# Closing weights' parts, block 0's splits and the last product of a fused attention and expert kernel: a change of order

## The chip, the cores and the metric

One core of a Trainium2 chip runs the whole kernel. The metric is the device time of one execution in microseconds (us). The engines are TensorE (PE, with its weight loads PEld), VectorE (DVE), ScalarE (ACT), GpSimd (POOL) and SyncE (SP), which here only issues DMAs. Each engine works through its own instructions in the order of the program and waits for others by semaphores.

## The reference

Three layers on 1536 tokens of 512 numbers, all in float32:

```python
attn = retention(q, k, v, lam)            # 2 x 8 heads x 768 x 64, blocks of 64 with decay
x = attn.transpose(0, 2, 1, 3).reshape(1536, 512)
logits = x @ w_gate                       # 8 experts
P = exp(logits - logits.max())
for _ in range(8):                        # Sinkhorn: rows, then columns
    P /= P.sum(1, keepdims=True) + 1e-09
    P /= P.sum(0, keepdims=True) + 1e-09
    P *= 1536 / 8
for e in range(8):                        # every token through every expert
    out += P[:, e:e + 1] * (relu(x @ w1[e]) @ w2[e])     # 512 -> 1024 -> 512
h = out @ w_in                            # 512 -> 2048
return (h - tanh(h)) @ w_out              # 2048 -> 512
```

## The kernel before, in words

Every float32 product is three products of halves: a factor is split into a high part (an ACT copy to fp32r, `split` with `which` 0) and a low part (a subtraction on DVE or POOL, `which` 1), both at L176 and L178, and high x high, low x high and high x low are added up in PSUM.

**Attention** takes some 60 us. **The expert layer** is a loop over 64 **slots** (from L838): a slot is one quarter of the hidden units of one expert (`q`) for one half of the tokens (`b`, six tiles of 128). The first matrix product of a slot is done by a scheme with seven block products (1, 2, 5, 6, 7, 4, 3 in that order on TensorE) on sums of blocks, and sums of the results; between them stands the second matrix product of the slot before, `tiles(s - 1, ...)`, six tiles, three after product 6 and three after product 7 (L617 to L641). DVE adds each tile to `yacc` at L641. The slot begins with ACT's copy `sa<-pal` (L858) of product 1. The relu of a result is an ACT copy (L679: `h0h`, `h1h`) and a DVE remainder (L680: `h0l`, `h1l`). Product 5 of the next slot goes into a PSUM bank that `h1l<-pal` of this slot was the last to read.

**Other work is hung into the slots** in four lists: `fd` runs behind the issue of product 5 and ACT's copy of it, ahead of product 6 and ACT's copy `sb`; `fa` behind product 7 and DVE's addition `pah`; `fb` behind the last tiles, ahead of the relu of `pah`; `fc` at the slot's end. The position sets an instruction's place in its engine's queue. The lists hold the expert weights (a load of `wraw` by SP in `fc`; POOL's `w_sum` in `fa` of even slots; `w1_split` in `fd` and `fa` and `w2_split` in `fb` of odd slots, with remainders of the last two on POOL), the gate and Sinkhorn in the early slots, the scaling `scale0` in slots 7 to 9, and the **conversion of the closing weights** in slots 5 to 60. These come as float64, in 64 pieces `n` of 128 x 256. `conv(u, i, j)` (L563) does step `j` of a piece:

- j = 0: SP loads the piece into a ring of three (`d`).
- j = 1: five DVE operations (L580 to L587, all on SBUF) and two POOL operations (L588, L589) make a float32 of it in a ring of seven.
- j = 2: two DVE operations (L591, L592).
- j = 3: a piece p = n % 8 of the second four, or one of the first three, is split into a high and a low **part** (`block`: an ACT copy and a POOL subtraction `hl` into a ring of five) and a write to the scratch memory `wscr` is noted in `stores`; for p = 3 POOL makes two sums instead.
- j = 4 and 5 (after p = 3 only): two parts each; j = 4 also two POOL sums.

`flush` issues the noted writes on SP's queue: at the start of each `conv` step those of earlier slots, and all of them where its argument is true. A piece has j = 0 in `fa`, j = 1 in `fa` of the next slot and j = 2 in its `fc`. In ten slots (10, 16, 22, 26, 32, 38, 42, 48, 54, 58) a second piece has j = 0 in `fd`, j = 1 in `fb` and j = 2 in the next slot's `fd`. The hanging is written out at L790 to L800.

**The closing layer** (from L960) runs 24 groups (3 blocks of 512 tokens, 8 quarters) of seven block products on 128 x 256 blocks `f`, with the function h - tanh(h) made on ACT and DVE in steps (`unit`), ending in a high part (`hi`, L952, ACT) and a low part (`lo`, L954, DVE, `gl`); `second` is the last matrix product. Block 0's input is made in slot 63 and after it: `turn` transposes, and `x2_parts` makes the sums (DVE, L716) and splits (ACT copy `x2h`, remainder `x2l`) in the order that calls at L802 to L807, L890, L892 and L973 give. The output tiles are evacuated by ACT and DVE in turn and written by `evac` (L662).

Of the kernel before, what the change touches and what calls it, by code (L numbers as in the profile page):

```python
# [17 lines left out]
B, H, S, D = 2, 8, 768, 64  # L18
E, DM, FE, FF = 8, 512, 1024, 2048
N = B * S  # L20
CH = 128
# [6 lines left out]
TPB = BT // 128  # L28
NU = 2 * E
NQ = FF // 512  # L30
# [6 lines left out]
NS = len(SLOTS)  # L37
# [18 lines left out]
def kernel(  # L56
# [85 lines left out]
    for g, (b, j) in enumerate(order):  # L142
        at_ = [w for w, (p, _) in kept.items() if p == j]
# [396 lines left out]
    def flush(all=False):  # L540
        while stores and (all or stores[0][0] < now[0]):
            stores.pop(0)[2]()
# [19 lines left out]

    def conv(u, i, j):  # L563
        q, p = 2 * u + i // 8, i % 8
        flush(j == 2)
        if j == 0:
            d = cq.tile([128, NC64, 2], I32, tag=f"d{count[2] % 3}", name=f"d{u}_{i}")
            count[2] += 1
            nc.sync.dma_start(out=d.rearrange("p n t -> p (n t)"),
                              in_=wio[u].bitcast(I32)[:, i * 2 * NC64:(i + 1) * 2 * NC64])  # L570
            c0 = cp.tile([128, NC64], I32, tag="c0", name=f"c0_{u}_{i}")
            box[q, p] = [d, c0]
            return
        if j == 1:
            box[q, p].append(cq.tile([128, NC64], I32, tag=f"c1_{count[0] % 7}", name=f"c1_{u}_{i}"))
            count[0] += 1
        d, c0, c1 = box[q, p]
        hi, lo, val = d[:, :, 1], d[:, :, 0], c1.bitcast(F32)
        if j == 1:
            nc.vector.tensor_scalar(out=c0, in0=hi, scalar1=3, scalar2=0x40000000,  # L580
                                    op0=ALU.logical_shift_left, op1=ALU.bitwise_xor)
            nc.vector.tensor_scalar(out=c1, in0=hi, scalar1=-0x80000000, scalar2=None, op0=ALU.bitwise_and)
            nc.vector.scalar_tensor_tensor(out=c0, in0=c0, scalar=0x7FFFFFFF, in1=c1,
                                           op0=ALU.bitwise_and, op1=ALU.bitwise_or)
            nc.vector.tensor_scalar(out=val, in0=lo.bitcast(U32), scalar1=2.0 ** -52,
                                    scalar2=None, op0=ALU.mult)
            nc.vector.tensor_scalar(out=lo, in0=c0, scalar1=-0x800000, scalar2=None, op0=ALU.bitwise_and)  # L587
            nc.gpsimd.tensor_tensor(out=val, in0=val, in1=lo.bitcast(F32), op=ALU.mult)  # L588
            nc.gpsimd.tensor_tensor(out=val, in0=val, in1=c0.bitcast(F32), op=ALU.add)  # L589
        elif j == 2:  # L590
            nc.vector.tensor_scalar(out=lo, in0=hi, scalar1=0x7FFFFFFF, scalar2=None, op0=ALU.bitwise_and)  # L591
            nc.vector.scalar_tensor_tensor(out=val, in0=lo.bitcast(F32), scalar=thr, in1=val,  # L592
                                           op0=ALU.is_ge, op1=ALU.mult)
        elif j == 3:
            if p < 3:
                block(q, (0, 256, 1536)[p], val)
            elif p == 3:
                a11, a22 = (box[q, k][2].bitcast(F32) for k in (0, 2))
                nc.gpsimd.tensor_tensor(out=a22, in0=val, in1=a22, op=ALU.add)
                nc.gpsimd.tensor_tensor(out=val, in0=a11, in1=val, op=ALU.subtract)  # L600
            else:
                block(q, 1792 + 256 * (p - 4), val, True)
        elif j == 4:
            a11, a12, a22 = (box[q, k][2].bitcast(F32) for k in range(3))
            block(q, WI[5], a22)
            block(q, WI[7], val)
            nc.gpsimd.tensor_tensor(out=a11, in0=a22, in1=a11, op=ALU.subtract)
            nc.gpsimd.tensor_tensor(out=a12, in0=a12, in1=a11, op=ALU.subtract)
        else:
            a11, a12 = (box[q, k][2].bitcast(F32) for k in range(2))  # L610
            block(q, WI[6], a11)
            block(q, WI[3], a12)
# [49 lines left out]
    def evac(b, t):  # L662
        if t == 0:
            yacc[b] = yp_.tile([128, TPB, DM], F32, tag=f"y{b}", name=f"yout{b}")
        y = yacc[b][:, t]
        if t % 2 == 0:
            nc.scalar.activation(out=y, in_=ypsum[b, t], func=ACTF.Copy)
        else:
            nc.vector.tensor_copy(out=y, in_=ypsum[b, t])
        n0 = t % B * S + (b * TPB + t) // B * CH  # L670
        (nc.scalar if t % 2 == 0 and b == NBLK - 1 else nc.sync).dma_start(out=out[n0:n0 + 128, :], in_=y)

    def scale0(c):
# [60 lines left out]
    fd, fa, fb, fc = spots  # L734

    def put(f, s, what, *a):
        f[s].append(lambda: what(*a))
# [51 lines left out]
    n = 0  # L789
    for s in range(lo_, hi_):  # L790
        more = s % 2 == 0 and (s - lo_) // 2 * extra // ((hi_ - lo_) // 2) != ((s - lo_) // 2 + 1) * extra // ((hi_ - lo_) // 2)
        for steps in (((fa, s - 1), (fa, s), (fc, s)), ((fd, s), (fb, s), (fd, s + 1)))[:1 + more]:
            for j, (f, at_) in enumerate(steps):
                put(f, at_, conv, n // (nconv // NQ), n % (nconv // NQ), j)
            at_ = (at_, at_ + 1)[f is fc]
            put(fa, at_, conv, n // (nconv // NQ), n % (nconv // NQ), 3)
            if n % 8 == 3:
                for j in (4, 5):
                    put(fa, at_ + j - 3, conv, n // (nconv // NQ), n % (nconv // NQ), j)
            n += 1  # L800
    assert n == nconv
    for k in range(KT):  # L802
        if k == 2:
            put(fb, NS - 1, x2_parts, (1, 0), (1, 1), 5)
        put((fa, fb)[k // 2], NS - 1, turn, 0, k)
    put(fb, NS - 1, x2_parts, (5, 0))
    put(fc, NS - 1, x2_parts, (5, 1), (2, 0), (2, 1), (3, 0))  # L807


    def product(ps, s, i, start):  # L810
# [78 lines left out]
    tiles(NS - 1, (0,))  # L889
    x2_parts(7, (3, 1))  # L890
    tiles(NS - 1, (1,))
    x2_parts(6, (6, 0), (6, 1))  # L892
    tiles(NS - 1, (2,))

    glos = [xp2.tile([128, 512], F32R, name=f"gl{i}") for i in range(2)]
# [66 lines left out]
    for g in range(ng):  # L962
        f = [bank(f"f{i}_{g}") for i in range(2)]
        ph[g, 0], ph[g, 1] = f
        c11, c12, c21, c22 = f[0][:, 0:256], f[0][:, 256:512], f[1][:, 0:256], f[1][:, 256:512]
        cproduct(g, c21, 1, True)
        nc.scalar.activation(out=s1, in_=c21, func=ACTF.Copy)
        unit(g - 1, 1, "t", "th", "q1")
        cproduct(g, c11, 2, True)
        unit(g - 1, 0, "p2")  # L970
        nc.vector.tensor_tensor(out=c11, in0=c11, in1=s1, op=ALU.add)
        if g == 0:
            x2_parts((7, 0), (7, 1), 4, (4, 0), (4, 1))  # L973
        unit(g - 1, 0, "cp")
        unit(g - 1, 1, "w", "sub")
        unit(g - 1, 0, "hi")
        unit(g - 1, 1, "q2")
        if g == 0:
            tiles(NS - 1, (3,))
        elif g == 1:  # L980
            turn(2, 0)
            turn(2, 1)
        seconds(g - 2, 1, (0, 1))
        unit(g - 1, 0, "lo")
        unit(g - 1, 1, "w1", "p2")
        cproduct(g, c12, 5, True)
        nc.scalar.activation(out=s1, in_=c12, func=ACTF.Copy)
        cproduct(g, c21, 6, False)
        nc.scalar.activation(out=s2, in_=c21, func=ACTF.Copy)
        unit(g - 1, 1, "mk")  # L990
        b, j = g // NG + 1, g % NG - 1
        if b < NBLK and j >= 0:
            if b == 2 and j == 0:
                x2_alloc(2)
            x2_step(b, j, nc.gpsimd)
        if g == 0:
            for k in range(KT):
                turn(1, k)
        elif g == 1:
            turn(2, 2)  # L1000
            turn(2, 3)
        seconds(g - 2, 1, (2, 3))
        for n, (_, _, p) in enumerate(loads):
            if p >= 0 and p == g - 2:
                w2_load(n)
        cproduct(g, c21, 7, False)
        nc.vector.tensor_tensor(out=c22, in0=c21, in1=s1, op=ALU.add)
        cproduct(g, c12, 3, False)
        nc.vector.tensor_tensor(out=c12, in0=c12, in1=s2, op=ALU.add)
        unit(g - 1, 1, "cp")  # L1010
        unit(g, 0, "t", "th")
        unit(g - 1, 1, "hi")
        unit(g, 0, "q1", "q2", "mk", "w")
        unit(g - 1, 1, "lo")
        unit(g, 0, "sub", "w1")
        if g == 0:
            tiles(NS - 1, (4,))
        seconds(g - 1, 0, (0, 1))
        cproduct(g, c21, 4, False)
        for n, (_, _, p) in enumerate(loads):  # L1020
            if p >= 0 and p == g:
                w1_load(n)
        if g == 0:
            tiles(NS - 1, (5,))
            w2_load(2)
        seconds(g - 1, 0, (2, 3))
    g = ng - 1
# [8 lines left out]
    second(g, 0, range(TPB), (0, 1))  # L1036
    second(g, 0, range(TPB), (2,))
    unit(g, 1, "hi", "lo")
    second(g, 1, range(TPB), (0, 1))
    for t in range(TPB):  # L1040
        second(g, 1, (t,), (2,))


# [43 lines left out]
```

## Time and profile before

| | |
|---|---|
| median of 3 runs | 1264.67 us (1263.93 to 1264.79) |
| the profiled execution | 1266.17 us, of which its span, first to last instruction, 1264.4 us |
| granted TensorE clock, mean | 0.999 |
| busy: DVE, ACT, POOL | 1022.3 us (81%), 591.7 (47%), 531.8 (42%) |
| DMA | 141.83 MB, 112 GB/s in the mean |
| largest waits of SP | for POOL's `w2l` 327.2 us (30 times), for DVE's `w1l` 229.9 (31), both ahead of the loads of `wraw`; for POOL's `hl` 135.2 (38), ahead of writes |

Busy shares are of the span. A time in the trace is in us from the span's start; durations of matmuls overlap, since they are pipelined, and a stretch between the starts of two of them tells the pace. "[3.78 <-DMA wscr<-hl]" behind a row means that the engine was idle for 3.78 us before it, and what ended that.

### The profile page before, as it was taken

To read this page: it belongs to the slowest core of one execution; us is meant where nothing else is said; L and a number is where in the kernel's file an instruction comes from. 1 tells how busy PE (TensorE), PEld (TensorE's weight loads), DVE (VectorE), ACT (ScalarE), POOL (GpSimd) and SP (SyncE) were. 2 spreads that over 40 slices of the span, in tenths; PEclk is the share of its full clock that TensorE was granted. 3 is DMA by queue.
4 is the path that set the end of the run, shared out by engine and by line. 5 is a ranking of instruction groups with operands and counts; after the bars stand their busy time and mean duration, and the time that the engine had idled before them with its cause. 6 is when DMAs were issued, how large, how long until landed. Compare 5 with 4: busy or idle time off the path is not lost. (4 is left out here: it accounts for less than half of the span.)

```text
span 1264.4 us, 20257 instructions
## 1 busy us (share of the span) xinstructions
PE 1237.5 (98%) x7450; PEld 1139.8 (90%) x7450; DVE 1022.3 (81%) x1914; ACT 591.7 (47%) x1191; POOL 531.8 (42%) x696
## 2 busy tenths in 40 slices
PE   8999999999999999999999999999999999999997
PEld 6889998899999999989999999999989899999996
DVE  6978888877888887887787888887785688888987
ACT  5653333333333433333333443333333378888875
POOL 4843444544554545554554554554452022031000
PEclk9999999999999999999999999999999999999999
DMA  9311122322222333232232222232325267284571
GB/s 332 121 34 42 51 67 67 109 68 75 84 84 76 95 109 105 76 95 81 76 100 76 84 83 76 67 102 87 111 57 194 92 205 254 101 276 150 198 260 67
DMA packets 63634, 141.83 MB, mean 112 GB/s; under 512 B 6064, under 2 KB 33200, under 8 KB 63536
## 3 DMA queue, kind: packets, MB, share of 16 engines
q1 hardware_dynamic: 63104, 140.02, 33.5%
q8 instruction: 58, 0.95, 0.3%
q10 hardware_dynamic: 432, 0.53, 0.1%
q14 instruction: 40, 0.33, 0.1%
HBM read 114.32 MB, written 26.21 MB: 111 GB/s over the span
## 5 line engine op out<-in xcount | busy, mean ns | idle before, releaser
L641 DVE SCALAR_TENSOR_TENSOR yacc<-yq,prob,yacc 128x512 f32<-128x512 f32 x336 | 239.5, 744 | 95.9 <-PE yq L628 95.4
L178 POOL TENSOR_TENSOR w1l<-wsum,w1h 128x256 fp32r<-128x256 f32 x124 | 88.6, 745 | 179.0 <-ACT w1h L176 164.8
L626 PE MATMUL yq<-w2h,h1h 128*128 128x512 f32 x384 | 146.2, 381 | 1.1 <-ACT h1h L679 1.1
L628 PE MATMUL yq<-w2h,h1l 128*128 128x512 f32 x384 | 145.7, 379 | 0.0
L627 PE MATMUL yq<-w2l,h0h 128*128 128x512 f32 x384 | 145.6, 379 | 0.0
L628 PE MATMUL yq<-w2h,h0l 128*128 128x512 f32 x384 | 145.6, 379 | 0.0
L626 PE MATMUL yq<-w2h,h0h 128*128 128x512 f32 x384 | 145.6, 379 | 0.0
L627 PE MATMUL yq<-w2l,h1h 128*128 128x512 f32 x384 | 145.6, 379 | 0.0
L818 PE MATMUL pal<-xsl,w1h 128*128 128x384 f32 x384 | 125.3, 326 | 0.5 <-DVE xsl L178 0.5
L816 PE MATMUL pal<-xsh,w1h 128*128 128x384 f32 x384 | 125.6, 327 | 0.0
L819 PE MATMUL pal<-xsh,w1l 128*128 128x384 f32 x384 | 125.2, 326 | 0.0
L679 ACT ACTIVATE h1h<-pah 128x384 fp32r<-128x384 f32 x64 | 31.3, 490 | 172.5 <-PE yq L627 161.2
L178 POOL TENSOR_TENSOR w2l<-wraw,w2h 128x512 fp32r<-128x512 f32 x64 | 82.7, 1313 | 6.5 <-ACT w2h L176 6.5
L588 POOL TENSOR_TENSOR c<-c,d 128x256 f32<-128x256 f32 x64 | 47.4, 740 | 88.8 <-DVE d L587 85.1
L628 PEld LDWEIGHTS yq<-w2h,h1l 128*128 128x128 f32 x384 | 72.6, 189 | 10.6 <-DVE h1l L680 0.4
L627 PEld LDWEIGHTS yq<-w2l,h0h 128*128 128x128 f32 x384 | 72.6, 189 | 10.3
L626 PEld LDWEIGHTS yq<-w2h,h0h 128*128 128x128 f32 x384 | 72.7, 189 | 10.2
L628 PEld LDWEIGHTS yq<-w2h,h0l 128*128 128x128 f32 x384 | 72.6, 189 | 10.2
L626 PEld LDWEIGHTS yq<-w2h,h1h 128*128 128x128 f32 x384 | 72.6, 189 | 8.3 <-ACT h1h L679 1.4
L864 ACT ACTIVATE sa<-pbh 128x384 f32<-128x384 f32 x64 | 31.4, 491 | 102.1 <-DVE pbl L862 90.0
L129 POOL TENSOR_TENSOR wsum<-wraw 128x256 f32<-128x256 f32 x31 | 22.6, 730 | 134.3 <-DMA wraw<-in_w 134.3
L627 PEld LDWEIGHTS yq<-w2l,h1h 128*128 128x128 f32 x384 | 72.7, 189 | 6.8
(228 smaller groups left out, 3680.3 us busy)
## 6 DMA issues: line engine op xcount, KB each, us to landing
wraw<-in_w SPq DMA_DIRECT2D x64, 512.0 KB, 5.0
wscr<-hl SPq DMA_DIRECT2D x88, 256.0 KB, 5.7
d<-in_wio SPq DMA_DIRECT2D x64, 256.0 KB, 5.4
w1h<-wscr SPq DMA_DIRECT2D x18, 768.0 KB, 4.5
w1l<-wscr SPq DMA_DIRECT2D x18, 768.0 KB, 6.0
w2h<-wscr SPq DMA_DIRECT2D x18, 512.0 KB, 3.8
w2l<-wscr SPq DMA_DIRECT2D x18, 512.0 KB, 4.8
qk<-in_qkv SPq DMA_DIRECT2D x11, 512.0 KB, 8.2
```

The lines of the kernel that those rows point to most:

```text
L129: eng.tensor_tensor(out=s1, in0=a21, in1=a22, op=ALU.add)
L178: eng.tensor_tensor(out=lo, in0=src, in1=hi.bitcast(F32), op=ALU.subtract)
L588: nc.gpsimd.tensor_tensor(out=val, in0=val, in1=lo.bitcast(F32), op=ALU.mult)
L626: nc.tensor.matmul(out=yp, lhsT=hi, rhs=pairs(w2h[q][:, i]), start=i == 1, stop=False)
L627: nc.tensor.matmul(out=yp, lhsT=hi, rhs=pairs(w2l[q][:, i]), start=False, stop=False)
L628: nc.tensor.matmul(out=yp, lhsT=lo, rhs=pairs(w2h[q][:, i]), start=False, stop=i == 0)
L641: nc.vector.scalar_tensor_tensor(out=y, in0=yp, scalar=prob[:, c, q // 4:q // 4 + 1], in1=y, op0=ALU.mult, op1=ALU.add)
L679: nc.scalar.activation(out=hi, in_=ps, func=ACTF.Relu)
L816: nc.tensor.matmul(out=ps, lhsT=w1h[q][:, ws], rhs=pairs(xh[:, k]), start=start and k == 0, stop=False, skip_group_check=True)
L818: nc.tensor.matmul(out=ps, lhsT=w1h[q][:, ws], rhs=pairs(xl[:, k]), start=False, stop=False, skip_group_check=True)
L819: nc.tensor.matmul(out=ps, lhsT=w1l[q][:, ws], rhs=pairs(xh[:, k]), start=False, stop=k == 1, skip_group_check=True)
L864: nc.scalar.activation(out=sa, in_=pbh, func=ACTF.Copy)
```

## The change

Three things are put elsewhere; no instruction is added or taken away.

1. Steps j = 3, 4 and 5 of a piece go from `fa` to `fd` of the same slot, those of a second piece from `fa` to `fb`. All noted writes are issued at step j = 1 (in `fa` or `fb`) instead of j = 2.
2. Block 0's splits: ACT's copy (5, 0) goes from `fb` to `fc`, where the copies (2, 0) and (3, 0) now stand ahead of the remainders (5, 1) and (2, 1); the split of sum 6 goes from ahead of the last slot's third tile to behind the first addition (`c11`) of group 0.
3. The very last product runs tile by tile, three matmuls each, instead of the two `hi` matmuls of all four tiles and then the four `lo` matmuls. The line of `n0` in `evac` moves up; it is arithmetic of the host.

```diff
     def conv(u, i, j):
         q, p = 2 * u + i // 8, i % 8
-        flush(j == 2)
+        flush(j == 1)
...
         for steps in (((fa, s - 1), (fa, s), (fc, s)), ((fd, s), (fb, s), (fd, s + 1)))[:1 + more]:
             for j, (f, at_) in enumerate(steps):
                 put(f, at_, conv, n // (nconv // NQ), n % (nconv // NQ), j)
-            at_ = (at_, at_ + 1)[f is fc]
-            put(fa, at_, conv, n // (nconv // NQ), n % (nconv // NQ), 3)
-            if n % 8 == 3:
-                for j in (4, 5):
-                    put(fa, at_ + j - 3, conv, n // (nconv // NQ), n % (nconv // NQ), j)
+            f, at_ = (fd, at_ + 1) if f is fc else (fb, at_)
+            for j in (3, 4, 5) if n % 8 == 3 else (3,):
+                put(f, at_ + j - 3, conv, n // (nconv // NQ), n % (nconv // NQ), j)
             n += 1
...
-    put(fb, NS - 1, x2_parts, (5, 0))
-    put(fc, NS - 1, x2_parts, (5, 1), (2, 0), (2, 1), (3, 0))
+    put(fc, NS - 1, x2_parts, (5, 0), (2, 0), (3, 0), (5, 1), (2, 1))
...
     tiles(NS - 1, (1,))
-    x2_parts(6, (6, 0), (6, 1))
+    x2_parts(6)
     tiles(NS - 1, (2,))
...
         if g == 0:
-            x2_parts((7, 0), (7, 1), 4, (4, 0), (4, 1))
+            x2_parts((6, 0), (6, 1), (7, 0), (7, 1), 4, (4, 0), (4, 1))
...
     unit(g, 1, "hi", "lo")
-    second(g, 1, range(TPB), (0, 1))
     for t in range(TPB):
-        second(g, 1, (t,), (2,))
+        second(g, 1, (t,))
```

## Rows read from the trace of the kernel before

**Rows 1.** The page's busy times: busy us, share of the span, instructions.

```profile
PE 1237.5 (98%) x7450; PEld 1139.8 (90%) x7450; DVE 1022.3 (81%) x1914; ACT 591.7 (47%) x1191; POOL 531.8 (42%) x696
```

**Rows 2.** Waits of TensorE: us in total, times, longest us.

```profile
PE pbh L816 <- DVE h1l L680: 8.5, 10, 1.7
```

**Rows 3.** Timeline of ACT: start and duration of L858 in slots 7, 14, 19, 61.

```profile
155.56 0.49 ACT L858 ACTIVATE sa<-pal 128x384 f32<-128x384 f32 x1 [1.76 <-PE pal L819]
...
262.36 0.49 ACT L858 ACTIVATE sa<-pal 128x384 f32<-128x384 f32 x1 [1.52 <-PE pal L819]
...
335.33 0.49 ACT L858 ACTIVATE sa<-pal 128x384 f32<-128x384 f32 x1 [1.51 <-PE pal L819]
...
956.48 0.49 ACT L858 ACTIVATE sa<-pal 128x384 f32<-128x384 f32 x1 [1.52 <-PE pal L819]
```

**Rows 4.** Timeline of slot 42: its start on ACT, and `h0l` on DVE.

```profile
676.57 0.49 ACT L858 ACTIVATE sa<-pal 128x384 f32<-128x384 f32 x1 [1.52 <-PE pal L819]
...
686.47 0.54 DVE L680 SCALAR_TENSOR_TENSOR h0l<-pbl,h0h 128x384 fp32r<-128x384 f32 x1
```

**Rows 5.** Timeline of slot 32 and the start of product 5 of slot 33.

```profile
526.85 0.49 ACT L858 ACTIVATE sa<-pal 128x384 f32<-128x384 f32 x1 [1.52 <-PE pal L819]
...
529.06 1.92 SPq L551 DMA_DIRECT2D wscr<-hl  x3
...
530.37 0.48 ACT L867 ACTIVATE sb<-pal 128x384 f32<-128x384 f32 x1
...
533.40 0.33 PE L816 MATMUL pal<-xsh,w1h 128*128 128x384 f32 x1
...
535.25 0.61 ACT L176 ACTIVATE hl<-c 128x256 fp32r<-128x256 f32 x1 [3.78 <-DMA wscr<-hl]
...
536.22 2.48 POOL L178 TENSOR_TENSOR hl<-c,hl 128x256 fp32r<-128x256 f32 x3
...
538.79 0.53 DVE L680 SCALAR_TENSOR_TENSOR h0l<-pbl,h0h 128x384 fp32r<-128x384 f32 x1
...
543.92 0.43 PE L816 MATMUL pbh<-xsh,w1h 128*128 128x384 f32 x1 [1.60 <-DVE h1l L680]
```

**Rows 6.** L583 and tile `hl` (ns min/median/max; DMA in us); two page groups (busy, mean, idle).

```profile
L583 DVE SCALAR_TENSOR_TENSOR c<-c,c x64: 424/426/891, 152.0 to 937.1; 128x256 int32<-128x256 int32 x64
...
L176 ACT ACTIVATE hl<-c x88: 407/418/612, 162.2 to 945.9; 128x256 fp32r<-128x256 f32 x88
L178 POOL TENSOR_TENSOR hl<-c,hl x88: 724/812/1097, 165.5 to 951.3; 128x256 fp32r<-128x256 f32 x88
...
DMA to landing us min/median/max: 2.4/5.7/7.5
...
L641 DVE SCALAR_TENSOR_TENSOR yacc<-yq,prob,yacc 128x512 f32<-128x512 f32 x336 | 239.5, 744 | 95.9 <-PE yq L628 95.4
...
L129 POOL TENSOR_TENSOR wsum<-wraw 128x256 f32<-128x256 f32 x31 | 22.6, 730 | 134.3 <-DMA wraw<-in_w 134.3
```

**Rows 7.** Timeline from slot 63 to group 0; then a window: engines' busy us, PEclk, DMA.

```profile
1000.47 0.75 ACT L176 ACTIVATE x2h<-raw 128x512 fp32r<-128x512 f32 x1 [0.79 <-DVE raw L716]
...
1002.03 0.48 PE L626 MATMUL yq<-w2h,h1h 128*128 128x512 f32 x1 [1.08 <-ACT h1h L679]
...
1008.27 0.87 ACT L176 ACTIVATE x2h<-raw 128x512 fp32r<-128x512 f32 x1 [4.62 <-DVE raw L716]
...
1010.92 0.38 PE L915 MATMUL f<-x2h,w1h 128*128 128x256 f32 x1 [1.86 <-DVE f L971]
...
1011.90:1015.90 4.00, 4.00 (x24) 4.00 (x23) 0.91 (x2) 1.96 (x5) 1.60 (x3) 0.57 0.00 0
```

**Rows 8.** Timeline of the end; landing of the output writes (us).

```profile
1256.29 0.69 DVE L954 TENSOR_TENSOR gl<-un_raw,h1l 128x512 fp32r<-128x512 f32 x1 [0.70 <-ACT h1l L952]
...
1258.13 1.03 PE L658 MATMUL yp<-w2h,gl 128*128 128x512 f32 x4
...
DMA to landing us min/median/max: 2.0/2.8/4.3
```

More of the change, by code (lines that the diff above doesn't have):

```diff
@@ L665, in evac @@
         y = yacc[b][:, t]
+        n0 = t % B * S + (b * TPB + t) // B * CH
         if t % 2 == 0:
@@ L669, in evac @@
             nc.vector.tensor_copy(out=y, in_=ypsum[b, t])
-        n0 = t % B * S + (b * TPB + t) // B * CH
         (nc.scalar if t % 2 == 0 and b == NBLK - 1 else nc.sync).dma_start(out=out[n0:n0 + 128, :], in_=y)
```

## The prediction

> **What bounds the kernel.** I read the busy table first: TensorE is busy 98% of the span [rows 1], so the time is its work plus the little that it waits. The list of its waits comes next: after the attention part the largest is `pbh` (product 5) waiting for the DVE remainder `h1l`, 8.5 us in 10 slots [rows 2]. The starts of the slots give the full price. Slots 7 to 60, which hold the conversion of the closing weights, take 956.48 - 155.56 = 800.92 us; the undisturbed slots 14 to 18 take 72.97 us, 14.594 each [rows 3]. 54 x 14.594 = 788.1, so **12.8 us** are lost in the conversion slots (a stalled product also refills its pipeline, hence more than 8.5).
>
> Slot 32 shows how [rows 5]. SP issues the three writes of slot 31's parts late, at 529.06, behind the weight load. ACT then wants to copy a new part into the same ring of five, and waits 3.78 us for a write to land; the relu copy `h0h` stands behind it. POOL's three remainders `hl` (2.48 us) run beside DVE's five conversion operations. DVE reaches `h0l` only 11.94 us after the slot's start (526.85 to 538.79), everything behind it is late, and product 5 of the next slot waits 1.60 us. So in a slot with two conversions `h0l` may start 10.3 us in (11.94 - 1.60); with one conversion some 1.7 later, as five DVE operations fewer stand behind it (below). Slot 42, also with two, reaches it after 9.90 us and its successor waits for nothing [rows 4].
>
> The DVE operations themselves show the second half. L583, one of the five, reads and writes SBUF and takes 0.42 us at best, 0.89 at worst [rows 6]; in slot 32 it ran inside POOL's three `hl`. L641, which reads PSUM, takes 0.74 in the mean of 336 [rows 6]. The other four of the five have one SBUF input; I put them at 0.3 to 0.35 undisturbed and all five at 1.7. One `hl` of 0.81 us beside the five operations thus costs DVE about 0.4.
>
> **The change, part by part.**
>
> *Parts behind product 5, writes in mid-slot.* No instruction is added. The ACT copies (0.42 each), POOL remainders (0.81 each) and POOL sums of a part move from behind the `pah` addition (fa) to behind product 5 (fd), some 4 to 5 us earlier; those of a slot's second conversion go behind tile 5 (fb). POOL has them done before the five operations start, unless it has much else: ahead of each `wsum` it now waits 134.3 us in 31 for the weights [rows 6], 4.3 a time. The writes move in SP's queue from behind `wraw`'s load to ahead of the next `d` load. SP now waits there for `hl`, and the `d` load behind it has until the next slot's five operations, a whole slot against a few us: cost nothing. A write landed 5.7 us after issue in the median, 7.5 at most [rows 6]; issued 5 to 9 us into a slot it is down by 17, and the copy that needs its ring place comes at about 14.6 + 3. So the waits of ACT (slots 12, 32, 52) go.
>
> What lies under the new place: ACT's `sb` copy comes up to three copies later, 3 x 0.42 = 1.3 us. In slot 32 it ended at 530.85 and product 7, which may overwrite `pal` only then, started at 533.40 [rows 5]: 2.55 us of cover. DVE in fd mostly reads PSUM; its weight remainders in odd slots read SBUF and may be slowed by some 0.4 to 0.8, while DVE waits 0.78 before each of the following sums (95.4 us in 122 waits) [rows 6].
>
> What stays: POOL's four `wsum` operations (0.73 each [rows 6]) come when `wraw` lands, and the moved work can push them into the five. Three parts with two sums take 3 x 0.81 + 2 x 0.75 = 4.0 us of POOL, from about 2.9 (after ACT's `sa` and the first copy) to 6.9; `wsum` then runs to 9.8, and the five start at 8.2 (slot 42's 9.90 less 1.7): 1.6 us of overlap, 0.8 of delay, `h0l` at 10.7, 0.4 past what slots with two conversions allow. I leave 0.4 each in slots 10, 38 and 58, 0.4 in 11 (POOL full there), 0.2 in 32, and 1.0 for the rest, above all slots 9 and 10 with block 0's scalings, which the change leaves: 2.8 of 12.8 remain, **gain 10.0 us**. Bounds: 4.6 if only the landing waits and what hangs on them go (slots 12, 13, 32 and 52), 12.8 if all goes.
>
> The rule that speaks against this is in the Trainium skill, "SBUF — State Buffer", section "SBUF: two separate sides": VectorE and GpSimd share a pair of ports as an exclusive lock, and whoever comes second is blocked for the other's whole instruction. L583's doubling agrees. By the rule the moved remainders would block DVE's weight remainders just as they blocked the five operations; what that gives is a rival below.
>
> *Block 0's sums and splits.* (a) ACT's copy `x2h` at 1000.47 waits 0.79 for a DVE sum and holds `h1h` back; TensorE then waits 1.08 [rows 7]. Behind the relus, that copy costs them nothing: gain 1.1. Three copies instead of two now stand ahead of `h0h` of the last slot, needed only for tiles 3 to 5; cover enough. (b) The copy at 1008.27 (0.87) and its remainder stand ahead of the first group's addition, for which TensorE waits 1.86 [rows 7]. Moved behind it, the addition loses 0.7 of remainder and about 0.9 of waiting for ACT in front: 1.6 of the 1.86. The remainder is next wanted by product 6 of group 0, one product later (0.7 us): 0.1 to 0.2 may come back. Net of both, 2.8. (c) From 1011.9 to 1015.9 the granted clock was 0.57, a mixture of full and half (2.4 and 1.2 GHz) [rows 7]; it fell right after the 1.86 of idleness and cost 4.00 x 0.43 = 1.7. With 0.3 to 0.5 idle I take it to stay up: the mean clock of 0.999 leaves no room for falls after the slots' waits of 1.6 us. What follows on DVE hangs on the group's additions and moves along. **Gain 4.5 us**, bounds 2.0 ((a), half of (b), the clock falls anyway) and 5.4.
>
> *Last product tile by tile.* Before, eight matmuls need only `h1l`, and four `gl` ones follow from 1258.13 at 0.215 spacing, so all four tiles end within 0.65 us and four writes queue up [rows 8]. After, the third matmul needs `gl`, which DVE has at 1256.29 + 0.69 = 1256.98; TensorE would be there at 1258.13 - 6 x 0.215 = 1256.84, so it loses 0.2. Tiles end 0.65 apart; the last evacuation no longer queues behind another (about 0.2), and the last write goes out alone: writes of this kind landed in 2.0 us at best, 2.8 in the median [rows 8], 0.8 less. **Gain 0.8 us**, bounds 0 and 1.3. The moved `n0` line is host arithmetic: nothing.
>
> **Sum.** 10.0 + 4.5 + 0.8 = 15.3. The profiled execution took 1266.17 with a span of 1264.4; it stands 1.50 over the median of the runs. Its span would be 1249.1, its time 1250.9; against the median, 1264.67 - 15.3 = **1249.4 us**.
>
> **The rivals.**
> *The window fills again.* POOL is delayed by the same work earlier, and `wsum` and `w1l` slide into the five operations, which stay doubled. For: POOL's work per slot is unchanged and in the fullest slots reaches past 8.2 us. Against: in slots with one part it is done with that long before. Only the landing waits go, 4.6: 1264.67 - 9.9 = 1254.8. Chance 0.14.
> *The clock falls anyway* in the first group, as DVE and ACT feed it sparsely there: 1.7 less, 1251.1. For: two waits remain possible. Against: the only fall seen follows the longest wait. 0.07.
> *The port lock in the new place.* Odd slots: one `hl` holds the weight remainder for up to 0.81; against it stand three waits of 0.78 on DVE, so it shows only where DVE is already late (39, 59 and 11): 3 x 0.81 = 2.4 less, 1251.8. The skill's page just named would have it so. 0.03.
> *Slower.* The copies in fd still meet a write that has not landed, and now `sb` stands behind them. With a wait like 3.78 and 1.3 of copies against 2.55 of cover, product 7 loses 2.5 us. It decides from six such slots on (15.3 / 2.5); in the twelve slots with three parts it would cost 30: 1279. Against: the writes go out half a slot earlier. 0.03.
> *Nothing comes of it*: DVE's work is the same and each stall moves to the next wait; 1264. Against: slot 42. 0.03.
>
> **How the numbers follow.** The forecast has the remaining 0.70. The sum of the upper bounds, 12.8 + 5.4 + 1.3 = 19.5, gives 1245.2; that of the refilled window with poor ends, 4.6 + 2.6 + 0.5 = 7.7, gives 1257.0. A measurement here tells about 0.2%, 2.5 us, from no change. Faster 0.94, same 0.03, slower 0.03.
>
> **What would show it.** Slots 10 to 13, 32/33, 38 to 40 and 58 to 60 near 14.6 us; no ACT wait of `hl` on a write; L583's maximum seen rarely; `h0l` about 10 us into every slot. No wait of TensorE above 0.5 at the first group and a clock of 1.00 there. Evacuations 0.65 apart at the end. Wrong would be TensorE waiting for `sb` at product 7, or the five DVE operations still near 3.5 us in total.

## The result and the profile after

The kernel after takes **1250.79 us** in the median (1250.11 to 1251.02, 4 runs), the kernel before 1264.47 beside it (1263.93 to 1264.79, 4 runs): a ratio of 0.9891, 95% interval 0.9874 to 0.9908. It is 13.7 us faster; 15.3 were forecast. The profiled execution of after is the fastest of its four, 1250.11 with a span of 1248.3. Below the change, line numbers of after are 3 lower.

The page's busy times, beside [rows 1]:

```profile
PE 1233.6 (99%) x7450; PEld 1138.0 (91%) x7450; DVE 995.8 (80%) x1914; ACT 589.8 (47%) x1191; POOL 536.9 (43%) x696
```

The counts of instructions are those of before. DVE does the same 1914 operations in 26.5 us less: some of them became shorter. TensorE's waits, beside [rows 2] (us in total, times, longest):

```profile
PE yp L655 <- ACT h1l L949: 1.1, 1, 1.1
PE pbh L813 <- DVE h1l L680: 0.9, 3, 0.4
...
PE f L912 <- DVE f L968: 0.5, 2, 0.3
```

The 8.5 us at product 5 have become 0.9, the 1.86 at the first group's addition 0.3, and the wait for `h1h` is gone from the list. The timeline of ACT at slots 7 and 61, beside [rows 3]:

```profile
155.04 0.49 ACT L855 ACTIVATE sa<-pal 128x384 f32<-128x384 f32 x1 [1.76 <-PE pal L816]
...
945.80 0.49 ACT L855 ACTIVATE sa<-pal 128x384 f32<-128x384 f32 x1 [1.51 <-PE pal L816]
```

945.80 - 155.04 = 790.76, less 54 x 14.594 = 788.08: a loss of 2.7 us in slots 7 to 60, where before lost 12.8. Slot 32 and its neighbour, the timeline beside [rows 5]:

```profile
520.83 0.49 ACT L855 ACTIVATE sa<-pal 128x384 f32<-128x384 f32 x1 [1.52 <-PE pal L816]
...
524.24 1.15 ACT L176 ACTIVATE hl<-c 128x256 fp32r<-128x256 f32 x3
...
524.73 2.13 POOL L178 TENSOR_TENSOR hl<-c,hl 128x256 fp32r<-128x256 f32 x3 [3.01 <-ACT hl L176]
...
525.49 1.91 SPq L551 DMA_DIRECT2D wscr<-hl  x3
...
529.00 0.73 POOL L133 TENSOR_TENSOR wsum<-wraw,wsum 128x256 f32<-128x256 f32 x1
529.10 0.81 DVE L580 TENSOR_SCALAR c<-d 128x256 int32<-128x256 int32 x1
...
530.15 0.42 DVE L583 SCALAR_TENSOR_TENSOR c<-c,c 128x256 int32<-128x256 int32 x1
...
531.19 0.55 DVE L680 SCALAR_TENSOR_TENSOR h0l<-pbl,h0h 128x384 fp32r<-128x384 f32 x1
```

ACT's copies run without a wait, POOL's remainders are done at 526.86, and the writes go out in mid-slot. Only the last `wsum` still overlaps the five operations, and L580 is the one that it doubles. `h0l` starts 10.36 us into the slot (11.94 before), and the next product 5 has nothing to wait for. The lines L583 and `hl` (ns min/median/max; landing in us) and two DVE groups (busy us, mean ns, idle), beside [rows 6]:

```profile
L583 DVE SCALAR_TENSOR_TENSOR c<-c,c x64: 424/426/853, 151.4 to 927.0; 128x256 int32<-128x256 int32 x64
...
L178 POOL TENSOR_TENSOR hl<-c,hl x88: 729/747/973, 160.8 to 935.6; 128x256 fp32r<-128x256 f32 x88
...
DMA to landing us min/median/max: 2.4/2.6/7.2
...
L592 DVE SCALAR_TENSOR_TENSOR c<-d,c 128x256 f32<-128x256 f32 x64 | 35.8, 560 | 6.7
...
L591 DVE TENSOR_SCALAR d<-d 128x256 int32<-128x256 int32 x64 | 34.8, 544 | 0.0
```

L583 took over 0.7 us 27 times before and 8 times after; its mean fell from 606 to 477 ns. But L591 and L592, the conversion's later DVE operations, rose from 474 and 499 to 544 and 560: part of the meeting moved. A write lands in 2.6 us instead of 5.7, now that it is issued in mid-slot and not right behind a weight load in SP's queue.

The transition (timeline, then a window with PEclk before the DMA share), beside [rows 7]:

```profile
989.78 2.42 ACT L176 ACTIVATE x2h<-raw 128x512 fp32r<-128x512 f32 x3
...
997.25 0.71 DVE L178 TENSOR_TENSOR x2l<-raw,x2h 128x512 fp32r<-128x512 f32 x1
...
997.40 0.38 PE L912 MATMUL f<-x2h,w1h 128*128 128x256 f32 x1 [0.31 <-DVE f L968]
...
997.60:1001.60 4.00, 4.00 (x37) 3.99 (x37) 3.64 (x6) 2.45 (x6) 3.35 (x4) 1.00 0.00 0
```

The three copies now follow the relus, the remainder `x2l` follows the addition, and the clock stays at full. The end (timeline), beside [rows 8]:

```profile
1241.18 0.69 DVE L951 TENSOR_TENSOR gl<-un_raw,h1l 128x512 fp32r<-128x512 f32 x1 [0.69 <-ACT h1l L949]
...
1241.52 0.38 PE L656 MATMUL yp<-w2l,h1l 128*128 128x512 f32 x1
...
1241.92 0.48 PE L658 MATMUL yp<-w2h,gl 128*128 128x512 f32 x1
...
1242.44 0.60 ACT L668 ACTIVATE yout<-yp 128x512 f32<-128x512 f32 x1 [1.30 <-PE yp L658]
...
1243.09 0.69 DVE L670 COPY yout<-yp 128x512 f32<-128x512 f32 x1 [1.22 <-PE yp L658]
```

`gl` costs TensorE 0.40 - 0.215 = 0.2, and the four evacuations start 0.65 apart, up to 1244.39.

The span can be cut into pieces for every kernel: the loss of slots 7 to 60 (worked out as above); from slot 61's `sa` to the first closing product; from there to the first second product (`yp`); from the first of the last twelve `yp` matmuls to the end. Between the last two pieces all spans agree within 0.03 (228.77 to 228.80).

| kernel (us) | span | loss, slots 7-60 | slot 61 to closing | closing to `yp` | end |
|---|---|---|---|---|---|
| before | 1264.38 | 12.85 | 49.78 | 21.27 | 8.08 |
| after | 1248.32 | 2.68 | 48.50 | 18.13 | 7.12 |
| e1 steps | 1259.31 | 8.16 | 49.79 | 21.26 | 8.07 |
| e2 writes | 1258.79 | 9.14 | 49.77 | 19.61 | 8.08 |
| e3 block 0 | 1259.52 | 12.35 | 48.50 | 18.09 | 8.07 |
| e4 last product | 1262.98 | 12.77 | 49.77 | 21.27 | 7.12 |
| e5 relus first | 1260.06 | 11.52 | 48.46 | 19.66 | 8.08 |
| e6 sums late | 1259.98 | 11.91 | 49.79 | 18.05 | 8.08 |
| e7 POOL beside | 1256.43 | 11.26 | 48.49 | 18.06 | 7.11 |
| e8 two sums in fc | 1247.34 | 1.37 | 48.50 | 18.09 | 7.13 |
| e9 before, no remainders | 1251.59 | 1.61 | 49.77 | 19.61 | 8.08 |
| e10 after, no remainders | 1246.18 | 0.21 | 48.47 | 18.10 | 7.11 |
| e11 after again | 1247.97 | 2.87 | 48.46 | 18.11 | 7.12 |
| e12 e8 again | 1247.13 | 1.28 | 48.50 | 18.05 | 7.12 |

From before to after: 10.2 in the conversion slots, 1.3 + 3.1 in the transition, 1.0 at the end, 0.5 ahead of slot 7, 16.1 in all. e3 to e6 leave slots 7 to 60 as they were before; their losses there, 11.5 to 12.8, beside 12.85, show how much these slots vary by themselves.

### The profile page after: what moved, and what is told of

It reads as the page before. It is cut to its first block, busy times and chain, and to the rows that moved or that the text cites. A ratio compares the mean times of both kernels' runs of the same rounds, so it can differ in the third digit from the quotient of the medians.

```text
span 1248.3 us, 20284 instructions
## 1 busy us (share of the span) xinstructions
PE 1233.6 (99%) x7450; PEld 1138.0 (91%) x7450; DVE 995.8 (80%) x1914; ACT 589.8 (47%) x1191; POOL 536.9 (43%) x696
## 5 line engine op out<-in xcount | busy, mean ns | idle before, releaser
L641 DVE SCALAR_TENSOR_TENSOR yacc<-yq,prob,yacc 128x512 f32<-128x512 f32 x336 | 240.1, 745 | 105.5 <-PE yq L628 104.9
L178 POOL TENSOR_TENSOR hl<-c,hl 128x256 fp32r<-128x256 f32 x88 | 71.1, 819 | 190.7 <-ACT hl L176 190.7
L178 POOL TENSOR_TENSOR w1l<-wsum,w1h 128x256 fp32r<-128x256 f32 x124 | 91.1, 765 | 31.5 <-ACT w1h L176 31.5
L679 ACT ACTIVATE h0h<-pbl 128x384 fp32r<-128x384 f32 x64 | 31.7, 496 | 110.4 <-PE yq L627 110.4
L628 PEld LDWEIGHTS yq<-w2h,h1l 128*128 128x128 f32 x384 | 72.6, 189 | 10.7 <-DVE h1l L680 0.4
```

The source lines that it names most:

```text
L178: eng.tensor_tensor(out=lo, in0=src, in1=hi.bitcast(F32), op=ALU.subtract)
L628: nc.tensor.matmul(out=yp, lhsT=lo, rhs=pairs(w2h[q][:, i]), start=False, stop=i == 0)
L641: nc.vector.scalar_tensor_tensor(out=y, in0=yp, scalar=prob[:, c, q // 4:q // 4 + 1], in1=y, op0=ALU.mult, op1=ALU.add)
L679: nc.scalar.activation(out=hi, in_=ps, func=ACTF.Relu)
```

## The experiments

**One part at a time.** e1 moves the steps alone, e2 the writes alone:

```diff
 e1_steps_only (against before)
-            ...      # the five lines that put these steps in fa, as in the change
+            f, at_ = (fd, at_ + 1) if f is fc else (fb, at_)
+            for j in (3, 4, 5) if n % 8 == 3 else (3,):
+                put(f, at_ + j - 3, conv, ..., j)
 e2_writes_only (against before)
-        flush(j == 2)
+        flush(j == 1)
```

> The kernel before with the steps j = 3 to 5 moved to fd and fb alone; all writes stay at j = 2, at the end of a slot. Theory (ports and landings): the five DVE operations are freed, so h0l comes near 10 us in the slots with one part; but a ring place is still being written when the next slot's copies want it, now ahead of sb: ACT waits of hl on a write, 3 to 5 us in 3 to 6 slots, and product 7 waiting for sb some 2 us there. Loss in slots 7 to 60 falls from 12.8 us to 5 to 9 us. Rival (landings alone matter): the five operations are not the bound, the loss stays at 12 us or grows.

> The kernel before with the writes issued at j = 1 alone; copies, remainders and sums of the parts stay behind the pah addition. Theory: ACT's waits on writes go (12.2 us in 4 before), and with them the loss of slots 12, 13, 32, 33 and 52, so the loss of slots 7 to 60 falls by about 4.6, from 12.8 to some 8; L583 is still slowed to 0.85 in a good part of the slots. Rival (landings alone): the loss falls to under 4 us.

e1: 1261.3 us, ratio 0.9976 (0.9966 to 0.9987), 4.7 us less loss. The five operations are short again (1.7 to 2.4 us in most slots with one conversion), but two slots became longer than any of before, 32 (16.85 us) and 52 (16.91). TensorE's waits and the timeline of slot 32 in e1:

```profile
PE pal L814 <- ACT sb L865: 4.0, 2, 2.1
```

```profile
529.26 0.43 ACT L176 ACTIVATE hl<-c 128x256 fp32r<-128x256 f32 x1 [4.03 <-DMA wscr<-hl]
529.60 0.47 ACT L865 ACTIVATE sb<-pal 128x384 f32<-128x384 f32 x1
...
530.12 0.43 PE L814 MATMUL pal<-xsh,w1h 128*128 128x384 f32 x1 [1.99 <-ACT sb L865]
```

This is the mechanism of the rival "Slower", which put it at 2.5 us a slot: a copy waits for a write ahead of `sb`, and product 7 for `sb`. It costs 2.3 a slot here (16.85 and 16.91 against 14.59), in two slots where three to six were expected, and only while the writes are late.

e2: 1260.75 us, 0.9972 (0.9961 to 0.9983), 3.7 less loss. Landing in e2, and what TensorE still waits at product 5:

```profile
DMA to landing us min/median/max: 2.4/2.5/4.1
```

```profile
PE pbh L816 <- DVE h1l L680: 5.2, 8, 1.2
```

No copy waits for a write any more; L583 is over 0.7 us 29 times, and the slots 33, 39 and 59 stay at 15.9 to 16.1. What e2 gains has another source than these waits. POOL in slot 32, timeline of before and then of e2:

```profile
533.34 0.73 POOL L129 TENSOR_TENSOR wsum<-wraw 128x256 f32<-128x256 f32 x1 [5.17 <-DMA wraw<-in_w]
...
535.52 0.73 POOL L133 TENSOR_TENSOR wsum<-wraw,wsum 128x256 f32<-128x256 f32 x1
```

```profile
529.07 0.73 POOL L129 TENSOR_TENSOR wsum<-wraw 128x256 f32<-128x256 f32 x1 [4.05 <-DMA wraw<-in_w]
```

The `hl` remainders stand behind `wsum`, and `wsum` waits for its weights. It starts 6.49 us into the slot in before and 5.36 in e2. The weight load that it waits for is issued at the same place (0.9 us into an even slot in the median of both), but took 4.7 us to land with writes issued right behind it and 4.0 in e2 without them (medians of the even slots 8 to 58). So `wsum` and the remainders come earlier and meet less of the five operations. This is read from the two traces; no run changes the landing alone.

Alone the parts give 4.7 and 3.7, together 10.2. Without the 4.6 us that the steps alone lose in slots 32 and 52, e1 would have given 9.3.

**The transition and the end.** e3 is the whole edit of block 0, e4 that of the last product, e5 and e6 the two halves of e3:

```diff
 e5_relus_first_only (against before)
-    put(fb, NS - 1, x2_parts, (5, 0))
-    put(fc, NS - 1, x2_parts, (5, 1), (2, 0), (2, 1), (3, 0))
+    put(fc, NS - 1, x2_parts, (5, 0), (2, 0), (3, 0), (5, 1), (2, 1))
 e6_sum6_late_only (against before)
-    x2_parts(6, (6, 0), (6, 1))
+    x2_parts(6)
-            x2_parts((7, 0), (7, 1), 4, (4, 0), (4, 1))
+            x2_parts((6, 0), (6, 1), (7, 0), (7, 1), 4, (4, 0), (4, 1))
 e4_last_only (against before)
-    second(g, 1, range(TPB), (0, 1))
     for t in range(TPB):
-        second(g, 1, (t,), (2,))
+        second(g, 1, (t,))
```

> The kernel before with block 0's splits reordered alone. Theory: from the start of slot 61 to the first product of the closing layer 1.1 to 1.3 us less, from there to its first second product 3.1 to 3.4 us less, of which about 1.7 is the clock that no longer falls (granted 1.00 in the first group); in all 4.4. Rival (the clock falls anyway, from sparse feeding): 2.7 and a clock near 0.57 over 4 us.

> The kernel before with the last product tile by tile alone. Theory: the last 12 matmuls start 0.1 to 0.3 us apart from before by the wait for gl, the evacuations come 0.65 apart, the last write lands in about 2.0 to 2.4 instead of 3.1 us; from the last product's first matmul to the end 0.8 to 1.0 us less than 8.1. Rival (the writes' landing hangs on TensorE's end alone): 0.2 us longer.

> The kernel before with the copy (5, 0) moved behind the last relus alone; sum 6's split stays ahead of group 0's addition. Theory: TensorE's wait of 1.08 for h1h goes and the closing layer begins 1.3 us earlier after slot 61 (48.5 instead of 49.8); TensorE still waits 1.9 or more for the addition, since DVE's queue in front of it is as long, so from there to the first second product nothing is gained: 21.3 if the clock falls, 19.6 if it does not (it did not in the run with the writes moved alone, with the same wait of 1.86).

> The kernel before with sum 6's split moved behind group 0's addition alone. Theory: the wait of 1.08 stays and the closing layer begins 49.8 us after slot 61; the wait for the addition falls from 1.86 to about 0.3 to 0.5, which is worth 1.5 us, and the clock stays at 1.00: 18.1 us from the first product to the first second product. Rival (the clock's fall has nothing to do with the wait): 19.8 or a fall elsewhere in the first group.

e3: 1260.74 us, 0.9971 (0.9959 to 0.9982), 1.28 and 3.18 less in its two pieces. e4: 1263.17, 0.9992 (0.9983 to 1.0001); its piece is 0.96 shorter, which the time alone doesn't tell from no change. e5: 1262.9, 0.9989 (0.9979 to 0.9999); 1.32 in the first piece. e6: 1261.64, 0.9979 (0.9969 to 0.9988); the 1.1 for `h1h` stays, the wait for the addition is 0.23.

The clock was the surprise. Here is the stretch of 4 us from the end of the wait for the first addition, in e1 (wait 1.86), e4 (1.86), e5 (1.90) and e2 (1.86), one fence each:

```profile
1005.84:1009.84 4.00, 4.00 (x21) 4.00 (x22) 1.20 (x2) 1.93 (x4) 2.58 (x3) 0.57 0.00 0
```

```profile
1010.46:1014.46 4.00, 4.00 (x21) 4.00 (x22) 1.20 (x2) 2.05 (x4) 2.59 (x3) 0.57 0.00 0
```

```profile
1008.24:1012.24 4.00, 4.00 (x36) 4.00 (x37) 2.50 (x4) 2.65 (x5) 2.58 (x3) 1.00 0.00 0
```

```profile
1006.96:1010.96 4.00, 4.00 (x36) 4.00 (x37) 2.50 (x4) 2.65 (x5) 2.59 (x3) 1.00 0.00 0
```

The wait and the work are the same (only e5 has other code ahead of it), and TensorE does 21 matmuls in one and 36 in the other. Before, e1 and e4 fell to half (1.2 GHz) for 3.4 us; e2, e5 and e9 did not. Where it fell the piece lasts 21.27, where not 19.61 to 19.66: the fall is 1.7 us, and the wait with all that follows it another 1.5 (19.6 to 18.1).

**What makes the five operations slow.** e7 puts eight small POOL additions beside them, released by DVE's third sum of the slot; e9 and e10 take POOL's remainder of the parts out of before and after and store the rounded copy twice, so that the closing weights' low parts are missing:

```diff
 e7_pool_beside (against after)
+        for i in range(8):
+            nc.gpsimd.tensor_tensor(out=t, in0=y[:, 64 * i:64 * i + 64],
+                                    in1=y[:, 64 * i:64 * i + 64], op=ALU.add)
 e9_before_no_rest (against before), e10_after_no_rest (against after)
-        ...      # the same split of every second column, where `pair` is set
-            split(t[:, 0], t[:, 1], src, nc.gpsimd)
+        nc.scalar.activation(out=..., in_=..., func=ACTF.Copy)
-    ... dma_start(out=wscr[q][:, :, o:o + m], in_=t.bitcast(F32))
+    ... dma_start(out=..., in_=t[:, 0:1].bitcast(F32).to_broadcast([128, 2, m]))
```

> The changed kernel with eight extra POOL additions of 128 x 64 in each of 54 slots, released by DVE's third sum and so running beside the five DVE operations; their result is not used. Theory (POOL beside DVE is what slows the five): L583's mean goes from 0.48 to 0.7 or more, the five operations from 1.75 to 2.7 or more in most slots, and the slots with two conversions lose 0.5 to 1.5 us each, so the loss of slots 7 to 60 goes from 2.7 to 8 or more. Rival (the five were slow for another reason, as DMA landings): L583 stays at 0.43 to 0.48 and the loss at 2.7.

> The kernel before with POOL's remainders of the converted parts (hl, 0.81 us each) left out: both halves of a stored part hold the rounded copy, so the closing weights' low parts are not computed. Places and writes are those of before. If it is the 0.81 us POOL remainder beside them that slows the five DVE operations, L583 falls from a mean of 0.61 to 0.48 or less and its operations of 0.8 are seen only where POOL's wsum or its sums of two parts run; the loss of slots 7 to 60 falls from 12.8 to between 4 and 7, as the waits of ACT for a write to land (slots 12, 32, 52) stay. Rival, the moved steps helped by their place on ACT and in DVE's order and not by POOL: L583 stays at 0.55 or more and the loss above 10.

> The kernel after with the same remainders left out (the closing weights' low parts are not computed). If what is left of the loss is POOL's work reaching into the five operations, the loss of slots 7 to 60 falls from 2.7 to 0.5 or less, and slots 12, 33, 39 and 59 come to 14.6. Rival, what is left comes from the wsum and w2l work that hangs on the weights' landing or from DVE itself: the loss stays at 1.5 or more.

e7: 1258.53 us, 0.9956 (0.9941 to 0.9971). The loss came back (11.26), but not by the way expected. POOL's groups and DVE's L583 and L592, which are L590 and L599 there:

```profile
L568 POOL TENSOR_TENSOR beside<-yacc 128x64 f32<-128x64 f32 x432 | 136.6, 316 | 30.5 <-DVE yacc L648 0.8
```

```profile
L599 DVE SCALAR_TENSOR_TENSOR c<-d,c 128x256 f32<-128x256 f32 x64 | 47.3, 738 | 7.2 <-POOL c L596 0.6
...
L590 DVE SCALAR_TENSOR_TENSOR c<-c,c 128x256 int32<-128x256 int32 x64 | 33.5, 523 | 2.2
```

With POOL full of 0.316 us additions, L590 has a mean of 523 ns where 700 or more were expected. Most of what came back sits behind the slots with two conversions (39 and 59: 16.04 each; 33: 18.52, with a fall of the clock after a wait of 1.97). In slots 32 and 38 the additions start only when `wsum` ends, beside the last of the five at most, and push POOL's other work to a later place (in slot 38 its next conversion operation starts at 12.63 instead of 10.77 us into the slot); L599 rises to 738. The test mixed two things and settles nothing on the five operations.

e9 is the clean one: 1253.38 us in its one run, loss **1.61**. Its group of L583 (there L580), ACT's waits and TensorE's at product 5:

```profile
L580 DVE SCALAR_TENSOR_TENSOR c<-c,c 128x256 int32<-128x256 int32 x64 | 31.0, 485 | 2.2
```

```profile
ACT hl L557 <- DMA wscr<-hl: 6.4, 3, 3.1
ACT hl L557 <- POOL wsum L132: 4.0, 1, 4.0
```

```profile
PE pbh L813 <- DVE h1l L677: 0.9, 1, 0.9
```

Places and writes are those of before, yet 11.2 of its 12.85 us are gone: they hang on POOL's remainders of 0.8 us. Not all of it is slower operations. DVE also waits for these remainders, at L582 4.7 us in 4 in the trace of before (e2: 3.2 in 4), most of it in slot 12, timeline of before:

```profile
242.52 0.84 DVE L582 TENSOR_SCALAR c<-d 128x256 int32<-128x256 int32 x1 [2.81 <-POOL hl L178]
```

Slot 13, the longest of before (16.76), follows. e9 takes these waits and the meeting beside DVE away together and does not tell their shares apart. L580 came to 485 ns, just over the 480 expected. The second half of the expectation fell: the copies in slots 12, 32 and 52 still wait 3.1 to 4.0 us (the list puts the one of slot 12 down to `wsum`), and the slots behind them are at 14.6. In the trace of before these waits held up nothing either. In slot 32 the copy that waited ends at 535.86, while POOL is in `wsum` until 536.25, and DVE works without a gap from 534.65 to `h0l`. In slots 12 and 52 too the first remainder starts as `wsum` ends (11.06 and 9.8 us into the slot). What sends the remainders into the five operations is `wsum`, ahead of them in POOL's queue; moved to `fd`, they run while POOL would wait for the weights. e10 (1247.96 in its one run) has a loss of 0.21: what after still loses hangs on the same remainder, directly or by what it pushes back on POOL.

**Where the rest sits, and a better version.** The 2.7 us of after show as four long slots, 12 (15.29), 33 (14.94), 39 (15.24) and 59 (15.33), each behind a slot whose `h0l` was late, and 0.16 in slot 7. (Slot 14 takes 14.87, which slot 15 with 14.32 gives back.) Slot 38 and the start of product 5 in slot 39, timeline of after:

```profile
608.74 0.49 ACT L855 ACTIVATE sa<-pal 128x384 f32<-128x384 f32 x1 [1.52 <-PE pal L816]
...
613.05 0.73 POOL L607 TENSOR_TENSOR c<-c,c 128x256 f32<-128x256 f32 x1
613.86 0.73 POOL L608 TENSOR_TENSOR c<-c,c 128x256 f32<-128x256 f32 x1
614.54 0.75 POOL L178 TENSOR_TENSOR hl<-c,hl 128x256 fp32r<-128x256 f32 x1
...
617.45 0.92 POOL L133 TENSOR_TENSOR wsum<-wraw,wsum 128x256 f32<-128x256 f32 x1
617.81 0.83 DVE L583 SCALAR_TENSOR_TENSOR c<-c,c 128x256 int32<-128x256 int32 x1
...
619.28 0.54 DVE L680 SCALAR_TENSOR_TENSOR h0l<-pbl,h0h 128x384 fp32r<-128x384 f32 x1
...
624.43 0.43 PE L813 MATMUL pbh<-xsh,w1h 128*128 128x384 f32 x1 [0.22 <-DVE h1l L680]
```

The part's work keeps POOL until 615.29, `wsum` follows until 618.37, and its end doubles L583. `h0l` starts 10.54 us into the slot, and slot 39 is 0.65 longer than an undisturbed one. The two sums L607 and L608, 1.5 us, stand ahead of `wsum` though nobody needs them soon. e8 moves them, and the two sums of step j = 3, to the end of the slot (`fc`); e12 is that kernel again, beside after (e11) on one chip:

```diff
 e8_sums_late, e12_sums_late_again (against after)
-            elif p == 3:
-                ...  # a22 = val + a22; val = a11 - val
+        elif j == 6:
+            ...      # the same two sums, put at (fc, at_)
+        elif j == 7:
+            ...      # a11 and a12 of step 4 (L607, L608), put at (fc, at_ + 1)
```

> The changed kernel with POOL's two sums of steps 3 and 4 moved from fd to the end of the slot (fc). Theory: in slots 10, 18, 38 and 58 wsum ends 1.5 us earlier and meets the five DVE operations less; the loss of slots 39 and 59 (0.65 and 0.74 in the changed kernel) goes, that of 11, 12 and 33 falls; loss of slots 7 to 60 from 2.7 to 1.0 to 1.6, so some 1.3 us faster than the changed kernel. Rival (what is left comes from ACT or the writes): no difference.

> The kernel after once more, unchanged, beside the next one on the same chip: 1250.0 to 1251.3, a loss of 2.2 to 3.2 us in slots 7 to 60, and TensorE's clock at 1.00 in the first closing group, as its longest wait there is 0.5. Rival, the clock falls there by chance: up to 1.7 longer.

> The kernel after with POOL's two sums of steps 3 and 4 moved from fd to fc, once more beside the kernel after on the same chip: 1.0 to 2.0 us under it. Rival, the 1.3 us less loss in its first profile was chance: within 0.5 of it.

e8: 1248.98 us, 0.9882 (0.9867 to 0.9897), loss 1.37. On one chip, after took 1250.0 (1249.54 to 1250.42; 0.9878, 0.9863 to 0.9892) and e12 1248.74 (1248.41 to 1249.37; 0.9868, 0.9852 to 0.9885): 1.26 less, with runs that don't overlap, and losses of 2.87 and 1.28. Slot 38's `h0l` is at 9.90 in e12, slots 12, 14 and 33 are at 14.6, 11, 39 and 59 at 14.9 to 15.0, and TensorE's list has no wait for `h1l` left. It is the fastest version found that leaves nothing out.

## Why the prediction was right, and where not

**Conversion slots: 10.0 forecast, 10.2 measured.** The reading of the fall was right in the main: e9 shows that it hangs on POOL's remainders, beside the five DVE operations or, as the text did not see, ahead of L582. So was the remainder of 2.8 (measured 2.7) and, by its rows, the working of slot 38: POOL's part work was to end 6.9 us into the slot and `wsum` at 9.8, the five to start at 8.2, `h0l` at 10.7; measured are 6.55, 9.63, 8.26 (L580 at 617.00) and 10.54. The single prices were rougher. What slots 38, 58, 11 and 32 leave behind shows in the slots after them as 0.65, 0.74, 0.70 and 0.35 (0.4, 0.4, 0.4 and 0.2 forecast), that of slot 10 as 0.06 (0.4), and the "rest" of 1.0 is about 0.2 (slot 7). A wait at product 5 costs more than itself, as the text said: slot 39 waits 0.22 and is 0.65 longer. The matmul behind the wait took 0.43 where others take 0.33; the other 0.3 is in no wait of the list.

The term that was wrong is the lower bound, 4.6 "if only the landing waits and what hangs on them go". It took those waits for a loss of their own, as did the reading of slot 32, where ACT's wait of 3.78 comes first. e2, which takes them away, gains 3.7, near the bound, but as far as the traces show by earlier weights; e9, which keeps three of them, loses nothing in the slots behind them.

**The port lock in the new place** (0.03) would have cost 2.4 in slots 11, 39 and 59. Its mechanism is there, in the timeline of slot 39 of after:

```profile
628.64 2.63 POOL L178 TENSOR_TENSOR hl<-c,hl 128x256 fp32r<-128x256 f32 x3 [3.53 <-ACT hl L176]
628.92 0.92 DVE L591 TENSOR_SCALAR d<-d 128x256 int32<-128x256 int32 x1
629.95 0.73 DVE L592 SCALAR_TENSOR_TENSOR c<-d,c 128x256 f32<-128x256 f32 x1
```

L591 took 0.92 and L592 0.73 beside POOL's `hl` (their means are 0.54 and 0.56), and `h0l` came 12.01 us into the slot. But one-conversion slots have that room, as the working said, and slot 40 is at 14.59; in slot 11, where DVE is later still (12.46), it adds to what slot 12 loses. The weight remainders `w1l` of DVE, which the rival would have blocked, kept their mean (583 ns, 581 before); in slots 11 and 39 they start ahead of the moved `hl`. The Trainium skill, "SBUF — State Buffer", section "SBUF: two separate sides", says that a VectorE operation with two SBUF inputs and a GpSimd operation that reads SBUF exclude each other, and whoever starts first holds the shared ports for its whole instruction. L583, with two such inputs, agrees: 0.83 beside `wsum`, 0.42 at best. e7, with POOL operations of 0.316 us, neither confirms nor refutes it.

**"It goes slower" was a real mechanism.** Without the earlier writes it costs 4.6 us in two slots (e1). The chance of 0.03 rested on the writes going out half a slot earlier, and that is what removed it: in after no copy waits for a write.

**Transition: 4.5 forecast, 4.4 measured.** (a) gave 1.28 against 1.1. (b), net of both, stood at 1.7 and gave 1.5; the wait left is 0.31, inside the 0.3 to 0.5 named. (c) gave 1.66 against 1.7 in this pair of profiles.

**End: 0.8 forecast, 0.96 measured**, with the 0.2 lost at `gl`.

**The sum against the median is what failed**, by 1.4 us (1249.4 forecast, 1250.8 measured). Against the profiled execution it held: 15.3 forecast, 16.1 measured, of which 0.5 lies ahead of slot 7, where one wait of TensorE for `xsl` (0.53) is in the trace of before and not of after, and comes again in e12, so by chance. The step that failed is the last one, "against the median, 1264.67 - 15.3". The text had noted that the profiled execution stood 1.50 above the median, and yet took all of (c) from the median, although a fall of the clock is just such a thing as raises one execution above the others. e2, e5 and e9 show that the same wait goes without a fall as often as with one. Taken from the profile alone, 1266.17 - 15.3 = 1250.9. That the run of the median had no fall is argued, not shown: only profiled runs have a clock by stretch. A mean granted clock is on record for 50 other runs of before. In 14 of them it is 1.000, which leaves no room for a fall of 3.4 us; these took 1262.15 to 1264.68, the other 36 1262.45 to 1267.48. A run of 1264.67 can thus be one without a fall or one with it. A second source is as open: of the five profiles that leave slots 7 to 60 as in before (before, e3 to e6), before has the largest loss there, 12.85 against 12.3 in the mean, so some 0.6 of the measured 10.2 may belong to that one execution too.

**The signs.** Waits of ACT, the clock, the evacuations and L583's maximum came as written; "`h0l` about 10 us into every slot" did not in ten of the 54, where it came 11.1 to 12.5 us in (11, 59 and 39 latest: 12.46, 12.17, 12.01), and slots 12, 39 and 59 stood at 15.2 to 15.3 where "near 14.6" was written, against the text's own 0.4 for each.

## What to carry to other kernels

When a DVE operation shows two durations in one trace, look at what POOL runs beside it, and move POOL's work to where DVE reads PSUM (L641 kept its mean, 744 and 745 ns, though the remainders now run beside it); then look at what POOL now does later because of it. When work sits in a bad place, look for what stands ahead of it in its queue: here `wsum`, waiting for weights. A wait on the list may cost nothing: before pricing it, see whether what follows it would have been free to start earlier. Subtract from the median only what every execution has; what a single profiled one shows, such as a fall of the clock, belongs to that one's own time.

## What the runs showed of the hardware

The granted clock after the same wait of 1.86 to 1.90 us, in the same place of the program, fell to half in three profiled kernels (before, e1, e4) and stayed full in three (e2, e5, e9), 1.66 us apart. A write of 256 KB landed in 5.7 us in the median when issued right behind a weight load in SP's queue (before), and in 2.5 to 2.6 when issued in mid-slot (e2, after); the load itself landed in 4.7 us with such writes behind it (before) and in 4.0 without (e2). Leaving one POOL operation of 0.8 us per part out of the kernel before took 11.2 us off the loss of slots 7 to 60 (e9), though POOL is busy 42% of the span [rows 1] and TensorE waits for none of these.
